# Another draw of the order table of a sparse-attention and gated-FFN kernel

## The chip, the cores and the metric

The kernel runs on one core of a Trainium2 chip, as one program. The metric is the device time of one execution in microseconds (us). The engines have short names here: PE (TensorE, matrix products and transposes), DVE (VectorE), ACT (ScalarE), POOL (GpSimd) and SP (SyncE, which here only issues transfers). POOL issues transfers too. The notes `u0` to `u7`, `x`, `g` and so on are the program's own names.

## The reference

Two layers stand one behind the other. The first is causal attention over 4 batches, 8 heads, 768 positions and 64 values per head. For each query only six chunks of 32 keys count. They are chosen by an upper bound, which is worked out from the minimum and the maximum of each chunk's keys.

```python
k_min = np.min(k_chunks, axis=3)
k_max = np.max(k_chunks, axis=3)
ub = np.sum(np.maximum(q * k_min, q * k_max), axis=-1)      # shapes cut
ub = np.where(causal, ub, -1000000000.0)
top_chunks = np.argsort(ub, axis=-1)[..., -top_k:]          # top_k = 6
scores = scale * np.matmul(q, k.transpose(0, 1, 3, 2))
scores = np.where(sel & (pos[:, None] >= pos[None, :]), scores, -1000000000.0)
attn = softmax(scores)
x = np.matmul(attn, v)                                      # to 3072 x 512
```

The second is a gated feed-forward layer on the 3072 tokens, from 512 to 1536 and back to 512.

```python
gate = 1.0 / (1.0 + np.exp(-(x @ w_gate)))
val = x @ w_val
return (gate * val @ w_out).astype(np.float32)
```

## The kernel before

**Units.** The tokens are cut into eight units of 384 tokens, three blocks of 128 each. Unit `u0` holds the first block of batches 0, 1 and 2, where no choice of chunks is needed. `u1` and `u2` hold the rest of batch 0 (and the first block of batch 3), `u3` and `u4` batch 1 (and one block of batch 2), `u5` to `u7` the rest.

**Stages of a unit.** Each stage is a few small operations with names of the form `kind_unit_part`.

- `first` (lines 560 to 650) does the first blocks. For a batch `b`: `kfT_b` and `qfT_b` turn keys and queries on PE, `kf16_b` and `qf16_b` copy them out of PSUM as half floats, `scf_b` makes scores, `expf_b_e` (ACT) exponentiates, `cmf_b_e` (POOL) applies the causal mask, `pvf_b_e` multiplies by the values, `rzf` and `xf` divide, `xpsf_b_e` turns the result and `xTf_b_e` copies it to `xT`, the input of the feed-forward layer. The loads are `kf0_b`, `kf1_b`, `qf0_b`, `qf1_b` (128 KB each) and `vf_b` (256 KB).
- `keys_wide` and `queries_wide` prepare `u1` and `u2`. The loads `k0_u1` to `k3_u1` and `q0_u1` to `q3_u1` bring 192 KB each. `kn` and `qn` copy a loaded piece, `kT` and `qT` turn it on PE, `kx` takes minimum and maximum, `kt` and `hk` put the keys in place for the scores, `qf`, `qm` (the positive part) and `hq` do the same for the queries. For the other batches `keys_blocks` and `turn_queries` do this with DVE's own transposes.
- `choose` makes the bounds: `ub` on PE, `ubn`, `mx` (the eight largest) and `ap` on DVE, then `apt`, and `hqm` copies the choice into the part of `hq` that adds a penalty to the scores. `hkp` fills the opposite part of `hk` with the pattern `epat` once, at the start.
- `attend` does, for each head, scores (`sc`), `exp` on ACT, the mask `cm` on POOL, and `pv`; `finish` divides and turns (`rz`, `x`, `xps`, `xT`).
- `ffn` does, for each of twelve parts of 128, a gate product `g`, `tanh`, a value product `v` and their product `hg` on DVE; `project_out` follows with `o0`, `o1`, `o2`, the copy `osb` and the store `out`. `u5` and `u6` share a version with fewer products (`ffn_pair`).

**Weights.** `w_gate`, `w_val` and `w_out` are loaded in three parts each (`wg0` to `wg2`, `wv0` to `wv2`, `wo0` to `wo2`, 512 KB each) by POOL. `after0` and `after1` are copies of one word on POOL, which read the second half of the queries of batch 1 and of batch 2. `wg0` and `wv0` depend on `after0`, the other parts on `after1` (lines 472 to 487 hold these). So the weights wait for the first loads.

**What sets the order.** All operations are first recorded in a `Plan`, with the buffers that they read and write. Nothing is scheduled by a rule then: `Plan.order` reads the string `ORDER`, one word per operation, and hands the operations out in that order. A word is the operation's name; `@ENGINE` names an engine where it isn't the first of those that the operation allows; after a colon stand the numbers of the buffers of a kind (PSUM banks among them) that the operation takes. Each engine runs its own operations in the order of the table and waits at each for what it needs; SP's loads run in the order of their words too. An operation that comes to a buffer later than another holds it from then on, so that the numbers set what has to wait for what.

Words of the same operations can be read in the table of either kernel: `qn_u1_2@POOL:4` is the copy of the third piece of `u1`'s queries, on POOL, into buffer 4 of its kind. At the end of the program the loop `for op in plan.order(): op.emit(op.engine)` emits all 1784.

Of the kernel before, what the change touches and what calls it, by code (L numbers as in the profile page):

```python
# [109 lines left out]
hq1_u1_2@POOL hq0_u1_2 qm_u1_3 v_u0_6:5 hq0_u1_3@DVE qf_u1_1 kcr_u1 tanh_u0_6 hg_u0_5 hq1_u1_3@POOL g_u0_7:7,3,7  # L110
hq1_u1_1@DVE qm_u1_1@ACT v_u0_7:6 hq0_u1_1@DVE tanh_u0_7 hg_u0_6 ub_u1:0,2 hg_u0_7 g_u0_8:4,0,8 ubn0_u1:0 ubn1_u1
v_u0_8:1 tanh_u0_8 ubm0_u1 k1_u2 ubm1_u1 v16_0_1 mx0_u1:0 g_u0_9:3,1,9 k2_u2 mx1_u1 v_u0_9:7 tanh_u0_9 g_u0_10:5,2,10
ap0_u1 ap1_u1 hg_u0_9 v_u0_10:6 tanh_u0_10 apt1_u1:0 g_u0_11:0,3,11 apt0_u1 hqm1_u1_2@DVE hqm1_u1_0@ACT v_u0_11:2
hqm0_u1_0@DVE tanh_u0_11 hqm0_u1_2@DVE sc_u1_0_1:4,3 sc_u1_1_0:3,0 hg_u0_10 exp_u1_0_1 sc_u1_0_0:7 o0_u0_0:5,0
# [5 lines left out]
exp_u1_4_1 kx1_u2_1:0 qn_u2_1@POOL:6 pv_u1_0 kf0_3:2 kt_u2_3:0 kx0_u2_2 hk0_u2_2@POOL pv_u1_3 exp_u1_4_2 qT_u2_0:7  # L120
rz_u1_0:0 hk0_u2_3 kf1_3 qn_u2_3:2 sc_u1_5_1:2,1 kx0_u2_3 hk1_u2_2@POOL sc_u1_6_2:6,3 o1_u0_1 qf_u2_0:1 kx1_u2_3
qn_u2_2@POOL:1 exp_u1_5_1 x_u1_0:0 hq1_u2_0@POOL qm_u2_0@ACT:0 qf0_3:3 qT_u2_2:7 v16_0_4 exp_u1_6_2 kx1_u2_2
sc_u1_4_0:0 hq0_u2_0 vf_3:4 sc_u1_5_2:2 qf_u2_2@DVE sc_u1_6_0:3 hk0_u2_1@POOL qT_u2_3:6 exp_u1_4_0 rz_u1_1:1 kT_u2_0:1
qm_u2_2 qT_u2_1:7 x_u1_1:1 hq1_u2_2@POOL qf_u2_3 o2_u0_1 kt_u2_0:2 cm_u1_4 qf_u2_1@DVE qf1_3 qm_u2_3@ACT kx1_u2_0
hq1_u2_3@POOL exp_u1_6_0 xps_u1_1:0,1 kx0_u2_0 k00_1:0 hq0_u2_1@POOL pv_u1_4:6 hq1_u2_1 sc_u1_5_0:5 osb_u0_1@DVE
hk1_u2_0@POOL sc_u1_6_1:7 xT_u1_1@ACT o0_u0_2:3,0 kcr_u2@POOL cm_u1_6 exp_u1_5_0 qm_u2_1 exp_u1_6_1 kfT_3:1
hq0_u2_3@DVE hq0_u2_2@DVE hk0_u2_0@ACT ub_u2:4,0 hk1_u2_3 kf16_3:4 cm_u1_5 exp_u1_5_2 out_u0_1 v16_0_5 vc_3@ACT
pv_u1_6:5 ubn1_u2:0 pv_u1_5 k01_1 sc_u1_7_0:7,2 ubn0_u2 sc_u1_7_2:1 sc_u1_7_1:2 mx1_u2:0 exp_u1_7_0 qfT_3:0 exp_u1_7_2
o1_u0_2 mx0_u2 cm_u1_7 exp_u1_7_1 qf16_3:5 ap1_u2 pv_u1_7 ap0_u2 o2_u0_2 apt1_u2:0 k10_1 rz_u1_3:0 rz_u1_2:1
hqm1_u2_0@DVE hqm1_u2_2@ACT scf_3:4,7,0 x_u1_3:2 sc_u2_4_2:1,3 osb_u0_2 xps_u1_0:2 x_u1_2:1 xps_u1_3:0 exp_u2_4_2  # L130
xT_u1_0 xps_u1_2:5 expf_3_1:1 xT_u1_3 sc_u2_7_2:3,2 xT_u1_2 expf_3_0 apt0_u2 sc_u2_7_1:6 cmf_3_1 g_u1_0:1,1,12
exp_u2_7_2 hqm0_u2_2@DVE exp_u2_7_1 v_u1_0:2 hqm0_u2_0@DVE out_u0_2 cmf_3_0 tanh_u1_0 k11_1 pvf_3_1:0 g_u1_1:7,2,13
hg_u1_0 rzf_3_1:0 pvf_3_0:5 v_u1_1:4 xf_3_1:0 tanh_u1_1 rzf_3_0:1 xf_3_0:2 sc_u2_3_0:3,0 sc_u2_3_2:6 hg_u1_1
xpsf_3_1:1,0 exp_u2_3_0 sc_u2_3_1:2 q00_1:1 xTf_3_1 xpsf_3_0:0 g_u1_2:7,3,14 exp_u2_3_2 xTf_3_0 cm_u2_3 exp_u2_3_1
# [15 lines left out]
o2_u1_1 hqm0_u3_0@DVE exp_u3_6_1 hqm0_u3_2@DVE sc_u3_1_2:1,0 sc_u3_0_2:0,1 osb_u1_1 sc_u3_0_0:2 out_u1_0 pv_u2_7  # L150
exp_u3_1_2 xps_u2_2:4 q00_2:1 xps_u2_1:7 rz_u2_3:1 exp_u3_0_2 xT_u2_2 sc_u3_5_2:5,2 exp_u3_0_0 x_u2_3:1 sc_u3_0_1:3
xT_u2_1 exp_u3_5_2 xps_u2_3:1 sc_u3_1_1:0 cm_u3_0 exp_u3_0_1 xT_u2_3 sc_u3_1_0:4 exp_u3_1_1 sc_u3_6_0:6 pv_u3_0:2
exp_u3_1_0 sc_u3_5_0:7 out_u1_1 kx1_2_0:0 k16_2_0:6 exp_u3_6_0 sc_u3_3_0:5,1 exp_u3_5_0 q01_2 o0_u1_2:1,1 cm_u3_1
# [1046 lines left out]
```

## Time and profile before

| what | value |
|---|---|
| three runs | 295.46, 293.73, 294.32 us |
| median | 294.32 us |
| profiled execution, span | 292.6 us |
| busy PE, DVE, ACT, POOL | 274.8, 219.8, 207.1, 94.6 us |
| first gate product (g_u0_0) | 22.71 us after the start |
| bytes moved by transfers | 32.69 MB |

The span runs from the first to the last instruction of one profiled execution; the runs' times contain what lies around it. Each engine's busy time is a sum over its instructions. The page's second part divides the span into 40 equal slices of some 7.3 us and gives each a digit, the busy share in tenths; the clock row gives the clock that PE was granted in the same way. Other views list the chain of work that ended last, the instructions in order of time, the busy time in chosen stretches, and the transfers by queue.

### The profile page before, as it was taken

Reading aid. Unit: us, or ns where it says so; the run is one execution under the profiler, and the core shown is the slowest. Engines: PE = TensorE matmul, PEld = TensorE weight load, DVE = VectorE, ACT = ScalarE, POOL = GpSimd, SP = SyncE. Lnnn points to the kernel's source line nnn. Section 1 sums busy time; section 2 is a strip of 40 time slices with the busy share of each in tenths; the row PEclk is TensorE's granted clock in tenths of the full one; section 3 lists DMA queues with packets and bytes.
Section 4 is the critical chain, followed back from the end, with each engine's and each line's share of the span. In section 5 each row is a group of like instructions: output and inputs, shape, how many; then the busy total and the mean of one; then the engine's idle time right before and its main releaser. Section 6 shows DMA issues by size and latency. Waiting matters only on the chain.

```text
span 292.6 us, 7019 instructions
## 1 busy us (share of the span) xinstructions
PE 274.8 (94%) x2644; PEld 175.0 (60%) x2644; DVE 219.8 (75%) x617; ACT 207.1 (71%) x425; POOL 94.6 (32%) x165
## 2 busy tenths in 40 slices
...
PEclk9985999999999999999999999999999999999999
...
GB/s 164 241 188 220 196 196 224 226 190 181 183 183 138 192 134 203 86 48 187 172 223 132 38 52 23 2 3 0 70 40 3 2 0 0 2 75 61 81 1 108
DMA packets 123377, 32.69 MB, mean 112 GB/s; under 512 B 111440, under 2 KB 120400, under 8 KB 123344
## 3 DMA queue, kind: packets, MB, share of 16 engines
...
## 4 chain that ended last, share of the span: by engine, by line
PE 83%; DMA 5%; ACT 4%; DVE 4%; POOL 2%; issue 1%; POOLq 0%
PE o_u L938 19%; PE v_u L907 16%; PE g_u L907 15%; PE sc_u L824 11%; PE pv_u L857 6%; DMA wv<-in_moe_w_val_dram 5%; PE sug_u5u L1016 3%; PE suv_u5u L1016 3%; PE ube_u L763 2%; ACT att_u L835 2%; PE xps_u L884 2%; PE srg_u5u L1016 1%; PE srv_u5u L1016 1%; DVE hko L331 1%; PE qT_u L662 1%
## 5 line engine op out<-in xcount | busy, mean ns | idle before, releaser
L835 ACT ACTIVATE att_u<-sc_u 128x512 f16<-128x512 f32 (+3 forms) x184 | 89.9, 549 | 15.1 <-PE sc_u L824 14.6
L919 DVE SCALAR_TENSOR_TENSOR hg_u<-gate_u,v_u 128x384 f16<-128x384 f16 x72 | 38.5, 542 | 33.7 <-PE v_u L907 25.2
L841 POOL TENSOR_SCALAR_AFFINE_SELECT att_u<-att_u 128x384 f16<-128x384 f16 (+1 forms) x56 | 29.3, 529 | 103.0 <-ACT att_u L835 100.8
L907 PE MATMUL v_u<-xT_u,wv 128*128 128x384 f16 x288 | 59.7, 331 | 2.5 <-DMA wv<-in_moe_w_val_dram 2.5
L907 PE MATMUL g_u<-xT_u,wg 128*128 128x384 f16 x288 | 59.9, 331 | 0.4 <-DVE xT_u L331 0.4
L938 PE MATMUL o_u<-wo,hg_u 128*128 128x512 f16 (+1 forms) x252 | 59.8, 376 | 0.0
L915 ACT ACTIVATE gate_u<-g_u 128x384 f16<-128x384 f32 x72 | 35.5, 493 | 28.6 <-PE g_u L907 21.8
L907 PEld LDWEIGHTS <-wv 128*128 128x128 f16 x288 | 27.8, 99 | 20.3 <-DMA wv<-in_moe_w_val_dram 3.2
L938 PEld LDWEIGHTS <-hg_u 128*128 128x128 f16 x264 | 24.6, 98 | 23.0 <-issue 0.6
L907 PEld LDWEIGHTS <-wg 128*128 128x128 f16 x288 | 27.4, 99 | 17.2 <-issue 2.5
L824 PE MATMUL sc_u<-hqo,hko 128*128 128x128 f16 (+2 forms) x220 | 28.5, 243 | 0.4 <-ACT att_u L835 0.4
L857 PEld LDWEIGHTS <-att_u 128*128 128x128 f16 x640 | 25.0, 98 | 5.5 <-issue 1.6
L857 PE MATMUL pv_u<-v,att_u 128*128 128x65 f16 x640 | 27.3, 193 | 0.0
L824 PE MATMUL sc_u<-hqe,hke 128*128 128x128 f16 (+2 forms) x220 | 26.4, 243 | 0.0
L947 ACT ACTIVATE osb_u<-o_u 128x512 f32<-128x512 f32 (+1 forms) x22 | 13.2, 599 | 18.6 <-PE o_u L938 18.6
L824 PEld LDWEIGHTS <-hke 128*128 128x128 f16 x220 | 16.8, 98 | 6.5 <-issue 0.4
L824 PEld LDWEIGHTS <-hko 128*128 128x128 f16 x220 | 16.5, 98 | 6.2 <-issue 1.2
L540 POOL CAST v<-v 128x512 f16<-128x512 f32 x23 | 15.0, 658 | 0.4 <-DMA v<-in_v_dram 0.2
L876 DVE TENSOR_TENSOR x_u<-pv_u,rz_u 128x384 f16<-128x384 f32 (+1 forms) x28 | 14.5, 527 | 0.2
L786 DVE MAX8 mx_u<-ubn_u 128x8 f32<-128x8 f32 (+16 forms) x152 | 12.5, 158 | 0.1
L714 DVE STREAM_TRANSPOSE kt<-k 128x768 f16<-128x768 f16 x12 | 11.5, 956 | 0.0
L548 DVE TRANSPOSE_TENSOR_REDUCE kx<-k 128x24 f32<-128x768 f32 x12 | 11.4, 947 | 0.0
(169 smaller groups left out, 446.8 us busy)
## 6 DMA issues: line engine op xcount, KB each, us to landing
...
```

The source lines that it names most:

```text
L540: plan.add(f"v16_{b}_{ib}", {POOL: pool(H * D)}, lambda e: nc.gpsimd.tensor_copy(v16[b % 2][:, ib, :, 0:D], at(t)), reads=[t], writes=[("v ...
L824: nc.tensor.matmul(at(t)[:, o:o + 128 * m], hk[b % 2][e_][:, p, 128 * jb:128 * jb + 128], hq[u.side][e_][:, p, 128 * x:128 * (x + m)], sta ...
L835: plan.add(f"exp_{u.name}_{h}_{y}", {ACT: act(n)}, lambda e, t=t, att=att, b0=b0, n=n: nc.scalar.activation(at(att)[:, b0:b0 + n], at(t), ...
L841: nc.gpsimd.affine_select(out=dv, in_=dv, compare_op=ALU.is_ge, fill=0.0, base=0, pattern=[[0, u.m], [1, 128]], channel_multiplier=-1)
L857: nc.tensor.matmul(at(pv)[:, last, x, :], at(att)[:, c:c + 128], v16[b % 2][:, jb, h, :], start=(jb == 0), stop=(jb == ib))
L876: plan.add(f"x_{u.name}_{p}", {DVE: dve(u.t)}, lambda e: nc.vector.tensor_tensor(at(x_).rearrange("p a (e d) -> p e a d", e=2), at(pv)[:, ...
L907: nc.tensor.matmul(at(t), w16[:, c, 128 * fb:128 * fb + 128], at(u.xt)[:, c, :], start=(c == 0), stop=(c == 3))
L915: plan.add(f"tanh_{u.name}_{fb}", {ACT: act(T)}, lambda e, g=g, gate=gate: nc.scalar.activation(at(gate), at(g), AF.Tanh, scale=0.5), read ...
L919: plan.add(f"hg_{u.name}_{fb}", {DVE: dve(T)}, lambda e, w_=w_, gate=gate, hg=hg: nc.vector.scalar_tensor_tensor(at(hg), at(gate), 1.0, at ...
L938: nc.tensor.matmul(at(o), hgs[c][1][1]()[:, 128 * tb:128 * tb + 128], wo16[:, fc, lo:hi], start=(c == 0), stop=(c == NFB - 1))
L947: nc.scalar.activation(at(osb)[:, lo:hi], at(o), AF.Copy, scale=0.5) if e == ACT
L1016: nc.tensor.matmul(at(t), left[i](c), right[i](c), start=first and c == 0, stop=c == 1, skip_group_check=not first)
```

## The change

Only the string `ORDER` is replaced. The words name the same 1784 operations; their order is different, 697 of them have other buffer numbers, and many have another engine. The rest of the program is the same, its lines one further down, since the new table has one line more.

By engine, the number of operations on POOL goes from 159 to 186, on DVE from 471 to 453, on ACT from 424 to 415. PE and SP have the same operations as before. Among the moves: eight `qm` go to POOL, which had none; POOL does eleven `hqm` where it did two; several `hq` go to POOL; of the copies `xT` eleven go from DVE to ACT and four the other way; of the copies `E` eleven go from ACT to DVE and six the other way; five `osb` go from ACT to DVE.

The start of both tables:

```diff
-vf1_3:0 kf0_0:0 ident kcr0 epat0:0 kf1_0 vf1_2:1 v10 ident16 ap1 epat qf1_0:1 ap0 qf0_0 hq1 kcr1 vf_0:2 hq0 v11
-kf1_1:3 hkp111 kf0_1 hkp110 hkp011@ACT kfT_0:0 qf1_1:4 hkp010 qf0_1 hkp000 hkp100@ACT qfT_0:1 kf16_0@DVE:2 vf1_1:3
-qf16_0:4 kxf0 hkp001@POOL hkf0@ACT kf1_2:5 kxf1:0 scf_0:2,3,1 v16_0_0 qf0_2:0 hkf1@ACT kcr_f kf0_2 hkp101 kfT_1:4
-expf_0_0 qf1_2 expf_0_1:2 after0 cmf_0_0 kf16_1@DVE:5 vf_1:1 qfT_1:5 cmf_0_1 vf_2:2 pvf_0_0:6 wg0 qf16_1:6 rzf_0_0:0
-pvf_0_1:7 xf_0_0:0 rzf_0_1:1 scf_1:1,0,3 wv0 xf_0_1:1 xpsf_0_0:2,0 expf_1_1:0 xTf_0_0 xpsf_0_1:3 expf_1_0 xTf_0_1
-cmf_1_1 cmf_1_0 k1_u1:0 k0_u1 kfT_2:4 k3_u1 after1 wg1 qfT_2:5 kf16_2:4 wv1 q0_u1 vc_1@ACT qf16_2@DVE:2 q2_u1 wg2
-pvf_1_0:6 pvf_1_1:7 k2_u1 rzf_1_0:0 scf_2:2,0,1 vc_2@ACT xf_1_0:2 wv2 q3_u1 rzf_1_1:1 expf_2_1:2 xpsf_1_0:3 xf_1_1:0
-wo0 xTf_1_0 expf_2_0 xpsf_1_1:1 xTf_1_1 cmf_2_1 cmf_2_0 pvf_2_1:4 q1_u1 kn_u1_1:5 rzf_2_1:0 wo1 pvf_2_0:5 v_0_1:3
-xf_2_1:1 kn_u1_0:6 kT_u1_1:6 rzf_2_0:1 xf_2_0:2 wo2 xpsf_2_1:7 kT_u1_0:0 kt_u1_1:0 xTf_2_1 kx0_u1_1 hk0_u1_1@ACT
-hk1_u1_1@POOL xpsf_2_0:3 xTf_2_0 kt_u1_0:1 kx1_u1_1:1 g_u0_0:2,0,0 hk1_u1_0 hk0_u1_0@ACT kx1_u1_0 v_u0_0:1 tanh_u0_0
...
-tanh_u0_2 v_u0_2:6 kt_u1_3:2 qT_u1_0:2 kx1_u1_3 hk0_u1_3@ACT hk1_u1_3@POOL g_u0_3:0,3,3 hg_u0_2 qf_u1_0:0 v_u0_3:1
-kx0_u1_3 qm_u1_0@ACT:0 hq0_u1_0@POOL hq1_u1_0 g_u0_4:4,0,4 tanh_u0_3 tanh_u0_4 hg_u0_3 qn_u1_2@POOL:4 v_u0_4:5 v_0_3:5
...
+ident q3_u1:0 kcr0 k3_u1 ident16 epat0:0 kf1_0:0 epat kf0_0 k1_u1 vf_0:1 qn_u1_3:0 qf0_0:2 qf1_0 vf_1:3 kfT_0:0
+kf0_1:4 kn_u1_1@POOL:1 qT_u1_3:1 v10 kf16_0:2 kf0_2:5 kn_u1_3@POOL:3 kT_u1_1:2 qf_u1_3@DVE:0 vf1_1:4 kf1_1 v16_0_0
+hkp110 kt_u1_1:0 qf1_2:0 hkp010@POOL qfT_0:3 hkp011@ACT kx0_u1_1 qf1_1:1 kxf0 qf0_1 kxf1:0 qf16_0:5 k0_u1
+hk0_u1_1@POOL q1_u2:1 scf_0:4,5,1 kf1_2 kfT_1:6 expf_0_1:2 after1 q0_u1 expf_0_0 cmf_0_1 q1_u1 kf16_1@DVE:6 qfT_1:7
+cmf_0_0 qf0_2 kx1_u1_1:1 kn_u1_0:0 after0 vf_2:2 vc_1 hkp100 pvf_0_1:1 kT_u1_0:0 q2_u1 wg0 kfT_2:3 qf16_1@DVE:1 k2_u1
+v_0_2:4 qm_u1_3@POOL:0 pvf_0_0:5 qn_u1_1:5 v_0_1:1 kT_u1_3:4 hq0_u1_3 wv0 scf_1:6,2,3 k1_u2 kt_u1_3@DVE:1 kcr_f@POOL
+expf_1_0 rzf_0_1:0 rzf_0_0:1 hq0 hkp000 cmf_1_0 qn_u1_2:0 kcr1 expf_1_1:1 xf_0_0:0 hq1_u1_3@POOL kx1_u1_3 qn_u2_1:3
+kf16_2:1 qT_u1_1:7 pvf_1_0:6 cmf_1_1 kx1_u1_0 hk1_u1_1@ACT kx0_u1_3 qT_u1_2:5 vf1_2:6 hkf0 vc_2@ACT xf_0_1:1 pvf_1_1:2
+wg1 rzf_1_0:0 xf_1_0:2 kt_u1_0@DVE:2 wv1 ap1 qf_u1_2@DVE qfT_2:3 qf16_2:5 qf_u1_1 scf_2:4,1,3 xpsf_0_1:6,0 qm_u1_1@ACT
+xpsf_0_0:3 qn_u1_0@POOL:0 xTf_0_0@ACT xpsf_1_0:7 expf_2_0 hk1_u1_3 hq0_u1_2@DVE xTf_0_1@ACT qT_u1_0:5 cmf_2_0
+expf_2_1:2 rzf_1_1:0 xf_1_1:1 hkp101@ACT kx0_u1_0 cmf_2_1 xpsf_1_1:3 pvf_2_0:4 xTf_1_0 rzf_2_0:0 wg2 pvf_2_1:6
+rzf_2_1:1 xf_2_1:0 kn_u1_2:4 wv2 xf_2_0:2 v_0_3:3 xpsf_2_1:1 xTf_1_1 qT_u2_1:2 xTf_2_1@ACT xpsf_2_0:0 wo0 qf_u1_0
+kT_u1_2:7 qm_u1_2@ACT qm_u1_0 kt_u1_2:0 xTf_2_0 k2_u2 kx1_u1_2 g_u0_0:6,0,0 ap0 kx0_u1_2 v_u0_0:4 hq0_u1_1@DVE
+kcr_u1@POOL g_u0_1:3,1,1 hk0_u1_3@POOL ub_u1:1,5 hkp001@POOL tanh_u0_1 tanh_u0_0 hq0_u1_0 hg_u0_0 v_u0_1:0 wo1
...
```

In the new table, seven turns of `u1` and `u2` (`kT_u1_3`, `kT_u1_2`, `qT_u1_0` to `qT_u1_3`, `qT_u2_1`) stand ahead of `g_u0_0` that stood behind it; `ub_u1` follows `g_u0_1` where it followed `v_u0_7`; and the loads of `first` and of `u1` are mixed.

More of the change, by code (lines that the diff above doesn't have):

```diff
@@ L110 @@
[L110 to L114, printed above, removed]
@@ L120 @@
[L120 to L124, printed above, removed]
@@ L125 @@
[L125 to L134, printed above, removed]
@@ L150 @@
[L150 to L153, printed above, removed]
-kx0_2_0 exp_u3_3_0 k16_2_2:4 pv_u3_1 kx1_2_1 k16_2_1@ACT:5 sc_u3_3_1:3 o1_u1_2 cm_u3_5 exp_u3_3_1 cm_u3_6 kt_2_2:2
@@ new lines @@
+qm_u2_0@ACT kf16_3@DVE:0 exp_u1_6_2 kcr_u2@POOL vc_3@ACT ub_u2:5,3 osb_u0_1@DVE xps_u1_2:1 pv_u1_6:6 ubn1_u2:0 v_0_5:4
+xT_u1_2@ACT scf_3:2,0,3 mx1_u2:0 pv_u1_7 hq1_u2_0 o0_u0_2:7,0 expf_3_0 ap1_u2 hk0_u2_2@ACT rz_u1_3:0 ubn0_u2 o1_u0_2
+cmf_3_0 apt1_u2:0 x_u1_3:1 v_0_4:1 hqm1_u2_2@ACT hqm1_u2_0 o2_u0_2 mx0_u2 q10_1:1 hk1_u2_2@POOL hq1_u2_3 xps_u1_3:4
+expf_3_1:2 ap0_u2 sc_u2_7_1:3,0 xT_u1_3 sc_u2_4_2:1,1 osb_u0_2 v_1_2:3 pvf_3_0:2 apt0_u2 sc_u2_7_2:5 g_u1_0:6,1,12
+k16_1_3:6 rzf_3_0:0 exp_u2_4_2 kx1_1_1:1 hqm0_u2_2@ACT v_u1_0:0 cmf_3_1 xf_3_0:0 exp_u2_7_2 g_u1_1:4,0,13 kx1_1_2
@@ new lines @@
+xps_u3_3:4 sc_u4_0_1:6 osb_u2_1@DVE xT_u3_3@ACT cm_u4_1 sc_u4_2_2:7 ub_u5:5,2 xT_u3_2 exp_u4_2_2 v16_2_4 ap1_u4
+exp_u4_0_1 cm_u4_2 exp_u4_0_3 apt1_u4 k16_3_1@ACT:5 sc_u4_1_1:4 hq0_u5_2@POOL kt_3_0:3 o0_u2_2:0,1 hqm1_u4_0 ubn0_u5:0
+pv_u4_0:1 o1_u2_2 kx0_3_2 sc_u4_1_3:7 sc_u4_4_0:6,2 hq0_u5_0 exp_u4_4_0 sc_u4_2_3:3 o2_u2_2 ubn1_u5 exp_u4_1_3
+mx0_u5:0 exp_u4_2_3 sc_u4_4_3:5 g_u3_0:6,1,17 osb_u2_2 exp_u4_1_1 v_u3_0:2 mx1_u5 out_u2_2 k16_3_3@ACT:4 out_u2_1
+sc_u4_4_2:7 g_u3_1:3,0,2 ap0_u5 v_3_4:2 hqm1_u4_2@DVE pv_u4_1 v_3_3:4 ap1_u5 tanh_u3_1 sc_u4_3_0:0 tanh_u3_0 rz_u4_0:0
```

264 lines of the change are left out of this document (139 added, 125 removed).

## The prediction

> **What bounds the kernel now.** I read the head of the page first, then its slices.
>
> ```profile
> span 292.6 us, 7019 instructions
> PE 274.8 (94%) x2644; PEld 175.0 (60%) x2644; DVE 219.8 (75%) x617; ACT 207.1 (71%) x425; POOL 94.6 (32%) x165
> PEclk9985999999999999999999999999999999999999
> ```
>
> TensorE (PE) is busy for 94% of the span, the other engines for at most 75%. The clock row names the exception: the fourth slice has half the clock. So I cut the span at the first gate product (22.7 us) and at the points where the pace changes. The columns are the length, then busy time of PE, PEld, DVE, ACT and POOL, the granted clock, the DMA share and GB/s.
>
> ```profile
> 0.00:22.70 22.70, 12.36 (x90) 9.13 (x91) 16.06 (x39) 13.78 (x21) 16.50 (x33) 0.94 0.94 199
> 22.70:30.60 7.90, 5.36 (x18) 2.34 (x18) 2.81 (x6) 1.89 (x4) 0.34 (x1) 0.52 1.20 215
> 30.60:66.60 36.00, 36.00 (x370) 23.75 (x369) 29.39 (x110) 28.73 (x70) 14.76 (x31) 1.00 1.09 206
> 66.60:170.00 103.40, 102.52 (x1110) 66.51 (x1116) 96.31 (x260) 84.84 (x169) 47.87 (x77) 1.00 0.79 148
> 170.00:190.00 20.00, 19.16 (x247) 12.18 (x232) 19.77 (x87) 15.34 (x31) 7.58 (x11) 1.00 0.07 25
> 190.00:252.60 62.60, 62.60 (x622) 41.39 (x621) 45.20 (x101) 49.01 (x107) 7.51 (x14) 1.00 0.04 14
> 252.60:289.40 36.80, 36.80 (x209) 19.73 (x206) 10.26 (x20) 13.25 (x26) 0.00 (x0) 1.00 0.15 58
> ```
>
> From 30.6 us on PE has no idle time but 0.88 us in the fourth row and 0.84 us in the fifth, 1.7 us together; in the fifth DVE is busy for 19.77 of 20 us. What a new order can gain or lose therefore lies in two places: before 30.6 us, and in whether the later rows stay full. The chain of waits and then the timeline show the early part (start, duration, what; in brackets the idle time before it and what ended it).
>
> ```profile
> 12.89 13.74 DMA wv<-in_moe_w_val_dram
> ...
> 28.14 1.28 PE g_u L907 x4
> 29.42 1.11 PE v_u L907 x4
> 33.13 0.65 PE v_u L907 x4
> 37.23 0.65 PE qT_u L662 x6
> ...
> 288.74 0.68 PE ob_u L938 x12
> ```
>
> ```profile
> 11.97 0.93 POOL L479 DMA_DIRECT2D wg<-in_moe_w_gate_dram  x1
> 22.71 1.44 PE L907 MATMUL g_u<-xT_u,wg 128*128 128x384 f16 x4 [0.38 <-DVE xT_u L331]
> 26.68 1.46 PE L907 MATMUL v_u<-xT_u,wv 128*128 128x384 f16 x4 [2.53 <-DMA wv<-in_moe_w_val_dram]
> ```
>
> The first gate product starts at 22.71, the first value product waits 2.53 us for its weights, and four products run at about half pace (1.44, 1.46, 1.28 and 1.11 where 0.65 is the full-pace price). From 22.71 to the end of PE's work at 289.42 are 266.7 us.
>
> **The change part by part.** The same 1784 operations remain, so PE's work is the same, and so is the code that each emits. Three things move.
>
> *First, PE's order at the start.* Ahead of g_u0_0 there now also stand kT_u1_3, kT_u1_2, qT_u1_0 to qT_u1_3 and qT_u2_1. Six transposes of 128 columns take 0.65 us (the qT_u row above), so six turns of three and one of two are 2.2 us of later work brought forward. The order after some 40 us of PE's work is nearly the old one: g_u1_0 and g_u7_0 stand behind the same amount of PE work to within 0.1 us, and the tail is unchanged.
>
> *Second, SP's queue.* The old order loaded the fifteen pieces for `first` (kf, qf, vf) ahead of u1's eight. The new one mixes them. q2_u1 is now the 23rd load, with 3776 KB up to its end, and its users come early: on ACT qn_u1_2 stands ahead of expf_1_1, and on PE qT_u1_2 stands ahead of pvf_1_1, qfT_2 and scf_2, and so ahead of everything that leads to g_u0_0. Before, qn_u1_2 ran on POOL and had nothing of `first` behind it. This is a new wait, and its queue is the path to the first weight product. When does q2_u1 land? The transfers in three windows (queue: packets, MB, share of the engines; 2 to 14, 16 to 24, 28 to 46 us):
>
> ```profile
> q1 hardware_dynamic: 10054, 2.81, 99.4%
> ```
>
> ```profile
> q0 software_dynamic: 1020, 1.02, 79.0%
> q1 hardware_dynamic: 920, 0.67, 35.7%
> ```
>
> ```profile
> q0 software_dynamic: 2813, 2.80, 91.4%
> q1 hardware_dynamic: 2811, 0.72, 29.9%
> ```
>
> q1 carries SP's loads, q0 the weights that POOL issues. Alone, q1 moves 0.234 MB/us from about 2 us on; beside the weights 0.084 with packets of 768 bytes (16 to 24) and 0.040 with those of 256 bytes (28 to 46). Free of weights, q2_u1's 3.87 MB would be in at 2 + 3.87/0.234 = 18.5 us. The first weight transfer waits for after1 and after0, which read qf_2 and qf_1; qf1_1 is now the 14th load (2.29 MB, in at 11.8). Behind it POOL still has two masks and a cast:
>
> ```profile
> 6.51 0.62 POOL L540 CAST v<-vf 128x512 f16<-128x512 f32 x1 [0.27 <-DMA vf<-in_v_dram]
> 13.86 1.22 POOL L620 TENSOR_SCALAR_AFFINE_SELECT attf<-attf 128x512 f16<-128x512 f16 x2 [0.22 <-ACT attf L618]
> ```
>
> So wg0's issue moves from 11.97 to about 11.8 + 1.22 + 0.62 = 13.7, and the crowding, which I put at 2.5 us behind the issue, to 16.2. By then q1 has moved 3.32 MB. What is left are 0.35 MB of 256-byte packets (vf_2 above all) and q2_u1's 0.20 MB. At 0.040 and 0.084 MB/us these take 8.7 and 2.3 us: 27.2. Undisturbed it is 18.5. I take the mean of the two crowded rates for the first part (0.062: 5.6 us), because only two weight transfers are in flight then where the row of 28 to 46 had more: L = 24.1.
>
> From that landing the chain to g_u0_0 runs through these durations (rows of the timeline, in the order of the new chain; a row of x2 holds two operations):
>
> ```profile
> 17.91 0.93 ACT L329 COPY kn_u<-kq_u 128x384 f32<-128x384 f32 x2
> 13.19 1.08 ACT L618 ACTIVATE attf<-scf 128x512 f16<-128x512 f32 x2 [1.18 <-DVE xf L635]
> 19.58 0.30 PE L627 MATMUL pvf<-vf,attf 128*128 128x65 f16 x4 [1.80 <-POOL attf L620]
> 14.25 1.06 PE L576 MATMUL qfT<-ident,qf 128*128 128x128 f32 x4
> 11.43 0.58 ACT L329 CAST qf<-qfT 128x512 f16<-128x512 f32 x1 [0.21 <-PE qfT L576]
> 12.40 0.61 PE L613 MATMUL scf<-qf,kf 64*128 64x128 f16 x8
> 16.95 0.28 PE L642 MATMUL xpsf<-ident,xf 128*128 128x128 f16 x2
> 4.14 1.47 ACT L329 COPY hko<-epat 64x1536 f16<-64x1536 f16 x1 [0.77 <-POOL epat L443]
> 20.38 0.88 PE L662 MATMUL kT_u<-ident,kn_u 128*128 128x128 f32 x3
> ```
>
> qn 0.47 (as kn), exp 0.54, mask 0.61, pvf 0.30, qfT 1.06, cast 0.58, scf 0.61, two xpsf 0.56. Then ACT, in its order, has two copies to xT (at most 0.48 each), two exps (0.54 each), the fill hkp101 (1.47) and kn_u1_2 (0.47). Last kT_u1_2, 0.88. The sum is 9.6; some fifteen hand-overs (scf ends at 13.01, its exp starts at 13.19) add about 0.9. So g_u0_0 starts at 24.1 + 10.5 = 34.6, not 22.71.
>
> *Third, engines.* Nine more of the `hqm` copies, eight `qm` and several `hq` go to POOL, some casts and copies change between ACT and DVE.
>
> ```profile
> L331 DVE COPY hqe<-apt_u 64x768 f16<-64x768 f16 x6 | 2.4, 394 | 0.1
> L333 POOL COPY hqo<-apt_u 64x768 f16<-64x768 f16 x1 | 1.1, 1082 | 1.6 <-DVE apt_u L797 1.6
> L333 POOL CAST hqe<-qf_u 64x768 f16<-64x768 f32 x5 | 4.2, 848 | 10.7 <-DVE qf_u L730 10.7
> ```
>
> An `hqm` costs 1.08 us on POOL and 0.39 on DVE. No row has `qm` on POOL; its bounds are 0.85 (the cast with the same columns) and twice that, and I take the upper, since the operation is another. By such prices some 25 us come onto POOL, 4 leave DVE and 7 ACT. POOL had 94.6 busy, so this lies beside PE's work as long as each copy is there before its scores. Where the cover ends, the third rival prices it. The gain is at most the 1.7 us that PE idled in the fourth and fifth rows, the loss bounded there; I take 1.2 of gain, nearer to its upper end because the idle time stands where DVE was full.
>
> **The sum.** Of the old 266.7 us, 2.5 go (the wait for wv0: now issued at about 15.7 and 13.74 on its way, it lands at 29.4, ahead of 34.6) and 2.7 (the four slow products: 0.79 + 0.81 + 0.63 + 0.46), and 2.2 were brought forward: 259.3. After a sparse start PE comes back at half clock as the second row of the stretches shows; four to five us at half pace, mostly filled, cost 2.0 (1 to 3). End of PE: 34.6 + 259.3 + 2.0 - 1.2 = 294.7, against 289.4: 5.3 later. That makes the span 297.9. The median of the runs, 294.32, lies 1.7 above the span, so the time is **299.6**.
>
> **The rivals.** *Crowding from the first byte.* The 28-to-46 row has as many packets on one queue as on the other (2813, 2811). If one weight transfer is enough for that share, L is 27.2, 3.1 later: 302.7. For it speaks the equality; against it that in 16 to 24 the counts were 1020 and 920 at other packet sizes, with q1 still at 0.084 MB/us. In the Trainium skill, "DMA: Bandwidth & Descriptors", section "Queues, rings and completion order", each DMA engine takes turns between the queues it has work for, a packet at a time; by that rule this rival holds, and the equal counts agree with it.
>
> *Faster.* If wg0's packets come later than I reckon, or q2_u1 passes before them, L is 18.5 and g_u0_0 starts at 28.1 to 29.0; then wv0, 13.74 us behind an issue at about 15.7, is just in. The end is 5.6 to 6.5 earlier than in my sum; with the whole 1.7 of idle time gained and 1 us of half pace it is 291.5 to 292.5. For it speaks that only 0.55 MB are in question, and that u1's own preparation, which PE, DVE and ACT must do anyway, then stands ahead of the weights' arrival. Against it: all sixteen DMA engines are busy from 2 us on, and this needs wg0's issue to slip by 2 us.
>
> *No change.* With L near 20 the two effects cancel: 295.
>
> *POOL becomes the bound.* In u1 to u4 the `hqm` on POOL is queued 1.2 to 1.5 us of PE work ahead of the scores that need it. If POOL is late there, nine copies at 0.7 us more and no relief elsewhere give 299.6 + 1.2 + 6.2/2 = 304. Against it: POOL's 47.87 of 103.40 us. In the Trainium skill, "SBUF — State Buffer", section "SBUF: two separate sides", POOL and some forms of DVE instructions hold a shared port one at a time, the other fully blocked. By that rule the 25 us more on POOL would also stretch DVE. The fourth row has DVE and POOL at 96.31 + 47.87 in 103.40 us, so at least 41 us lie side by side, if a blocked instruction isn't counted as busy.
>
> That the table might do nothing is excluded: the order of every queue differs.
>
> **How the numbers follow.** Forecast 0.44 (its own range 297 to 302), crowding from the first byte 0.14, POOL 0.1: slower 0.68. Faster 0.2. No change 0.12. About 0.5% is what a measurement of this kernel can tell. The range holds 8 in 10 if it reaches from the faster case's lower half to between the two late ones: 291.5 to 304.
>
> **What would show it.** In the changed kernel's trace: q2_u1 landing near 24; qn_u1_2 on ACT waiting for that DMA, and behind it a stretch of 4 to 8 us in which PE has little work; g_u0_0 near 34.6, with three or four products slower than 0.65 behind it, and no wait for wv0; hardly any idle time of PE after 45 us. It would be wrong if g_u0_0 started before 30 us, if PE had gaps of more than 2 us in the stretch that was full, or if a score waited for a copy on POOL.

## The result, and the profile after

| kernel | median | spread | ratio to before (95% interval) |
|---|---|---|---|
| before | 294.02 us (4 runs) | 293.73 to 295.46 | 1 |
| changed | 298.07 us (4 runs) | 296.65 to 298.5 | 1.0136 [1.0097, 1.0174] |
| changed, measured again with the last experiments | 297.15 us (7 runs) | 294.06 to 298.11 | 1.0093 [1.0059, 1.0128] |

The changed kernel is about 1% slower. The ratios leave out the few runs that were clearly slower than the others of the same kernel; the longest, 480 us at a mean granted clock of 0.57, is one of the kernel without seventeen copies on POOL, below. The head of its page and its clock row, to be held against those of before:

```profile
span 295.5 us, 6996 instructions
PE 275.5 (93%) x2644; PEld 176.7 (60%) x2644; DVE 215.6 (73%) x599; ACT 200.3 (68%) x416; POOL 122.2 (41%) x192
PEclk9995699999999999999999999999999999999999
```

DVE has 4 us less, ACT 7 us less, POOL 28 us more, and the span is 2.9 us longer. The fourth slice still shows half the clock, and now the fifth shows 0.6 of it. The busy time in stretches (columns as above: length, PE, PEld, DVE, ACT, POOL, clock, DMA share, GB/s), cut at the first gate product, which now starts at 32.49:

```profile
0.00:32.49 32.49, 17.27 (x110) 13.05 (x111) 17.75 (x41) 17.01 (x31) 19.44 (x37) 0.82 1.03 211
32.49:40.20 7.71, 7.71 (x66) 3.95 (x66) 5.13 (x22) 2.26 (x6) 3.10 (x5) 0.87 1.21 221
40.20:70.00 29.80, 29.59 (x301) 19.45 (x300) 22.67 (x80) 24.69 (x59) 15.78 (x33) 1.00 0.93 166
70.00:100.00 30.00, 28.68 (x292) 18.49 (x290) 27.40 (x76) 22.09 (x45) 15.86 (x25) 1.00 1.03 192
100.00:170.00 70.00, 70.00 (x745) 45.91 (x744) 61.61 (x172) 55.60 (x115) 45.50 (x63) 1.00 0.68 133
170.00:190.00 20.00, 20.00 (x281) 12.70 (x280) 17.90 (x67) 14.88 (x28) 11.27 (x12) 1.00 0.11 41
```

Up to the first gate product PE now has 17.27 us of work in 32.49 us, where it had 12.36 in 22.70, and the mean clock of that stretch is 0.82 instead of 0.94. After it PE is full but for 0.21, 1.32 and, further on, 0.04 us: 1.6 us, about the 1.7 of before. The chain of waits names what came last in the start, and the timeline shows the instructions at that place:

```profile
13.76 8.28 DMA kq_u<-in_q_dram
...
32.49 1.44 PE g_u L908 x4
...
291.66 0.68 PE ob_u L939 x12
```

```profile
13.85 0.99 POOL L480 DMA_DIRECT2D wg<-in_moe_w_gate_dram  x1
15.85 0.81 POOL L481 DMA_DIRECT2D wv<-in_moe_w_val_dram  x1
...
22.11 0.51 ACT L330 COPY qn_u<-kq_u 128x384 f32<-128x384 f32 x1 [3.86 <-DMA kq_u<-in_q_dram]
22.53 0.59 ACT L619 ACTIVATE attf<-scf 128x512 f16<-128x512 f32 x1
22.68 0.50 PEld L663 LDWEIGHTS qT_u<-ident,qn_u 128*128 128x128 f32 x3 [3.43 <-ACT qn_u L330]
22.68 0.90 PE L663 MATMUL qT_u<-ident,qn_u 128*128 128x128 f32 x3 [3.31 <-ACT qn_u L330]
23.02 0.40 ACT L330 COPY qn_u<-kq_u 128x256 f32<-128x256 f32 x1
23.25 0.64 POOL L621 TENSOR_SCALAR_AFFINE_SELECT attf<-attf 128x512 f16<-128x512 f16 x1 [3.67 <-ACT attf L619]
```

q2_u1 was issued at 13.76 and landed 8.28 us later, at 22.04. ACT stood idle for 3.86 us ahead of qn_u1_2, PE for 3.31 ahead of qT_u1_2, POOL for 3.67 ahead of cmf_1_1: one late transfer holds three engines, because its user stands in the middle of the chain of `first` on two queues. From there the chain runs to g_u0_0 without a longer pause.

The account of the two profiled executions: g_u0_0 starts 9.78 us later (32.49 against 22.71); from there to PE's end are 259.85 us (292.34 - 32.49) instead of 266.7, 6.85 less. The difference is the 2.9 us of the spans.

### The profile page after: what moved, and what is told of

Same layout as the page of the kernel before. It is cut to its first block, busy times and chain, and to the rows that moved or that the text cites. A ratio compares the mean times of both kernels' runs of the same rounds, so it can differ in the third digit from the quotient of the medians.

```text
span 295.5 us, 6996 instructions
## 1 busy us (share of the span) xinstructions
PE 275.5 (93%) x2644; PEld 176.7 (60%) x2644; DVE 215.6 (73%) x599; ACT 200.3 (68%) x416; POOL 122.2 (41%) x192
## 4 chain that ended last, share of the span: by engine, by line
PE 84%; DMA 5%; SPq 4%; ACT 2%; POOL 2%; issue 1%; DVE 1%; ACTq 0%; DVEq 0%; POOLq 0%
PE o_u L939 21%; PE g_u L908 15%; PE v_u L908 15%; PE sc_u L825 11%; PE pv_u L858 6%; DMA kq_u<-in_q_dram 3%; PE suv_u5u L1017 3%; PE sug_u5u L1017 3%; PE ube_u L764 3%; SPq L504 2%; DMA q<-in_q_dram 2%; PE xps_u L885 2%; PE srg_u5u L1017 1%; PE srv_u5u L1017 1%; POOL qm_u L565 1%; SPq L515 1%
## 5 line engine op out<-in xcount | busy, mean ns | idle before, releaser
L836 ACT ACTIVATE att_u<-sc_u 128x512 f16<-128x512 f32 (+3 forms) x184 | 92.1, 547 | 22.6 <-PE sc_u L825 20.0
L842 POOL TENSOR_SCALAR_AFFINE_SELECT att_u<-att_u 128x384 f16<-128x384 f16 (+1 forms) x56 | 28.5, 519 | 82.4 <-ACT att_u L836 68.8
L920 DVE SCALAR_TENSOR_TENSOR hg_u<-gate_u,v_u 128x384 f16<-128x384 f16 x72 | 37.6, 543 | 30.7 <-PE v_u L908 15.6
L916 ACT ACTIVATE gate_u<-g_u 128x384 f16<-128x384 f32 x72 | 34.2, 497 | 21.3 <-PE g_u L908 18.7
L825 PE MATMUL sc_u<-hqo,hko 128*128 128x128 f16 (+2 forms) x220 | 30.1, 243 | 0.0
L825 PE MATMUL sc_u<-hqe,hke 128*128 128x128 f16 (+2 forms) x220 | 29.1, 243 | 0.0
L948 ACT ACTIVATE osb_u<-o_u 128x512 f32<-128x512 f32 (+1 forms) x17 | 9.9, 590 | 19.8 <-PE o_u L939 19.8
L825 PEld LDWEIGHTS <-hko 128*128 128x128 f16 x220 | 17.4, 98 | 7.1 <-issue 0.5
L565 POOL TENSOR_SCALAR qm_u<-qf_u 128x768 f32<-128x768 f32 (+3 forms) x8 | 14.1, 1766 | 5.6 <-DVE qf_u L731 3.5
L731 DVE STREAM_TRANSPOSE qf_u<-q 128x384 f32<-128x384 f32 (+2 forms) x28 | 11.2, 436 | 3.3 <-DMA q<-in_q_dram 3.3
```

Source lines behind the costliest of these rows:

```text
L565: (nc.vector if e == DVE else nc.gpsimd).tensor_scalar_max(o, i, 0.0)
L825: nc.tensor.matmul(at(t)[:, o:o + 128 * m], hk[b % 2][e_][:, p, 128 * jb:128 * jb + 128], hq[u.side][e_][:, p, 128 * x:128 * (x + m)], sta ...
L836: plan.add(f"exp_{u.name}_{h}_{y}", {ACT: act(n)}, lambda e, t=t, att=att, b0=b0, n=n: nc.scalar.activation(at(att)[:, b0:b0 + n], at(t), ...
L842: nc.gpsimd.affine_select(out=dv, in_=dv, compare_op=ALU.is_ge, fill=0.0, base=0, pattern=[[0, u.m], [1, 128]], channel_multiplier=-1)
L916: plan.add(f"tanh_{u.name}_{fb}", {ACT: act(T)}, lambda e, g=g, gate=gate: nc.scalar.activation(at(gate), at(g), AF.Tanh, scale=0.5), read ...
L920: plan.add(f"hg_{u.name}_{fb}", {DVE: dve(T)}, lambda e, w_=w_, gate=gate, hg=hg: nc.vector.scalar_tensor_tensor(at(hg), at(gate), 1.0, at ...
```

## The experiments

All times are medians; ratios are to the kernel before, measured beside each. An edit names the words of the table that are moved.

**A load exchanged.** SP's queue alone is changed.

```diff
-... expf_0_1:2 after1 q0_u1 expf_0_0 ...
+... expf_0_1:2 after1 q2_u1 expf_0_0 ...
-... pvf_0_1:1 kT_u1_0:0 q2_u1 wg0 ...
+... pvf_0_1:1 kT_u1_0:0 q0_u1 wg0 ...
```

> The changed kernel with two words exchanged in the table: q2_u1 takes the place of q0_u1 in SP's queue (19th load, 3008 KB to its end) and q0_u1 the 23rd. In the changed kernel q2_u1 landed at 22.04 us, qn_u1_2 ran at 22.11 and g_u0_0 started at 32.49. If the late load is what the start waits for: q2_u1 lands at 2 + 3.08/0.234 = 15.2, qn_u1_2 runs at about 18.3 behind expf_1_0 and doesn't wait; the next late load is q0_u1 at about 22 for qn_u1_0, from whose end 6.0 us led to g_u0_0: g_u0_0 at 28.6, the time 3.9 us shorter than the changed kernel's, 294.2. If the start is bound by the work brought forward (the turns on PE) or by the weights instead, g_u0_0 stays above 31 and the time within 1.5 us of 298.1.

Measured: 292.62 us, 0.9962 [0.9941, 0.9983], span 291.1. The rows of its timeline:

```profile
17.77 0.51 ACT L330 COPY qn_u<-kq_u 128x384 f32<-128x384 f32 x1
...
22.40 0.50 POOL L334 COPY qn_u<-kq_u 128x384 f32<-128x384 f32 x1 [0.37 <-PE scf L614]
...
28.22 1.44 PE L908 MATMUL g_u<-xT_u,wg 128*128 128x384 f16 x4
```

qn_u1_2 runs at 17.77 with no wait ahead of it, g_u0_0 starts at 28.22 (28.6 was expected), and the span is 4.4 us shorter than the changed kernel's. That the late load held the start is shown; the sum that gave 28.6 is not. It ran over q0_u1, which landed at 22.28, but the chain of waits in this profile doesn't pass there: it runs from the landing of q1_u1 (16.36) over its copy and the masks on POOL. Two words decide whether the new table is slower than the old one or, by 0.4%, faster.

**The load one place later.**

```diff
-... kT_u1_0:0 q2_u1 wg0 kfT_2:3 qf16_1@DVE:1 k2_u1 ...
+... kT_u1_0:0 k2_u1 wg0 kfT_2:3 qf16_1@DVE:1 q2_u1 ...
```

> The changed kernel with q2_u1 and k2_u1 exchanged in SP's queue, so that q2_u1 is the 24th load, one load of 192 KB later. If its landing sets the start one for one: it lands at about 24.2 (2.2 us later, the pace of such loads beside the weights), g_u0_0 starts at 34.7, and the time is about 2.2 us longer, 300.3. If the start has another bound, g_u0_0 stays within 0.7 us of 32.49 and the time is the changed kernel's.

Measured: 298.99 us, 1.0168 [1.0124, 1.0212], span 297.6. From the chain of waits:

```profile
15.44 8.96 DMA kq_u<-in_q_dram
...
34.86 1.44 PE g_u L908 x4
```

The landing moved to 24.40, g_u0_0 to 34.86, the span by 2.1 us. The median rose by 0.9 us only, where 2.2 were expected; the profiles show the step more plainly than the times, because the landing differs from one execution to the next. Over the runs in which q2_u1 is the gate, the distance from the start of qn_u1_2 to that of g_u0_0 doesn't change at all: 22.11 to 32.49 (10.38) in the changed kernel, 24.47 to 34.86 (10.39) here, 20.88 to 31.27 (10.39) in the changed kernel's second profile, 22.02 to 32.42 (10.40) in the experiment on qm_u3 below.

**The users exchanged instead of the loads.** SP's queue is the changed kernel's; the words of piece 0 and piece 2 change places for qn, qT, qf and hq0, with their engines.

```diff
-... cmf_1_0 qn_u1_2:0 kcr1 ... qT_u1_2:5 ... qf_u1_2@DVE ... qn_u1_0@POOL:0 ... qT_u1_0:5 ... qf_u1_0 ...
+... cmf_1_0 qn_u1_0:0 kcr1 ... qT_u1_0:5 ... qf_u1_0@DVE ... qn_u1_2@POOL:0 ... qT_u1_2:5 ... qf_u1_2 ...
```

> The changed kernel with its loads as they are, but the early users exchanged: qn, qT, qf and hq0 of piece 0 take the places of those of piece 2, so that the operation on ACT ahead of expf_1_1 needs q0_u1 (landed at 16.06 in the changed kernel) and q2_u1 (22.03) is needed only by the copy on POOL behind wv1. If the place of the late load's user is what cost the time, this gives the same as moving the load: g_u0_0 near 28.3, the time 4 to 5 us shorter than the changed kernel's 298.1, q2_u1 still landing near 22. If the transfers themselves or the work brought forward cost it, the time stays within 1 us of the changed kernel's.

Measured: 293.2 us, 0.9961 [0.9929, 0.9994], span 291.3; g_u0_0 at 27.76, q2_u1 landing at 21.68. The load is nearly as late as before, and PE's first gate product is 4.7 us earlier: its user now runs on POOL at 22.51, without a wait, and of `first` only the masks of batch 2 stand behind it there. So a late landing costs this time only through the place of its user in the queues.

**The weights held back.** wg0 and wv0 stand behind cmf_1_1 on POOL.

```diff
-... kT_u1_0:0 q2_u1 wg0 kfT_2:3 ... hq0_u1_3 wv0 scf_1:6,2,3 ... cmf_1_1 kx1_u1_0 ...
+... kT_u1_0:0 q2_u1 kfT_2:3 ... hq0_u1_3 scf_1:6,2,3 ... cmf_1_1 wg0 wv0 kx1_u1_0 ...
```

> The changed kernel with wg0 and wv0 on POOL moved behind cmf_1_1, so that no weight is on its way while q2_u1 is. If the weights' packets are what slows q2_u1, it lands at about 18.5 instead of 22.04, with the same queue ahead of it; if the queue alone makes it late, it stays within 0.5 us of 22. The weights then come later: wg0 issued near 20.4, in at 28 to 30, wv0 at 30 to 33, so g_u0_0 starts at 29 to 30 and v_u0_0 may wait for wv0; the time is 0 to 3 us shorter than the changed kernel's.

Measured: 296.83 us, 1.0078 [1.0039, 1.0117]. The timeline of this kernel:

```profile
18.06 0.51 ACT L330 COPY qn_u<-kq_u 128x384 f32<-128x384 f32 x1
...
28.86 1.46 PE L908 MATMUL g_u<-xT_u,wg 128*128 128x384 f16 x4 [0.48 <-DMA wg<-in_moe_w_gate_dram]
33.23 1.46 PE L908 MATMUL v_u<-xT_u,wv 128*128 128x384 f16 x4 [2.90 <-DMA wv<-in_moe_w_val_dram]
```

With the same queue ahead of it, q2_u1 landed at 17.98 and its user didn't wait; the weights on their way made it 4 us late. But now the weights are late: v_u0_0 waits 2.90 us for wv0, the wait that the old table had too. The interval of the ratio overlaps the changed kernel's, so no gain is shown. The transfers between 18 and 22 us, the changed kernel first:

```profile
q0 software_dynamic: 521, 0.52, 78.1%
q1 hardware_dynamic: 687, 0.40, 37.9%
```

```profile
q1 hardware_dynamic: 3537, 1.05, 109.5%
```

Beside the weights SP's queue got 0.40 MB through in these 4 us, without them 1.05 MB.

**Two copies off POOL.** qm_u3_0 and qm_u3_2 back on DVE and ACT.

```diff
-... hg_u1_5 qm_u3_2@POOL:0 tanh_u1_7 ... k10_2 qm_u3_0@POOL rz_u2_1:0 ...
+... hg_u1_5 qm_u3_2@ACT:0 tanh_u1_7 ... k10_2 qm_u3_0 rz_u2_1:0 ...
```

> The changed kernel with qm_u3_0 and qm_u3_2 back on the engines that they had before (DVE and ACT; 0.72 and 0.86 us there, 1.80 us each on POOL in the changed kernel). In the changed kernel PE is idle for 1.3 us between 70 and 100 us, ahead of ub_u3, and the chain of waits runs through the load of q_1 (landing at 87.1), then qm_u3 on POOL twice. If POOL's price makes that gap, it goes away and the time is 1.3 us shorter, 296.8. If the load of q_1 makes it, more than 0.8 us of the gap stay. If DVE and ACT are too full to take the two, the time stays or grows by up to 0.5.

Measured: 297.97 us, 1.0106 [1.0059, 1.0153]. In 85 to 95 us (the changed kernel, then this one):

```profile
85.00:95.00 10.00, 8.68 (x95) 4.70 (x92) 7.92 (x22) 6.72 (x13) 6.95 (x9) 1.00 1.02 178
```

```profile
85.00:95.00 10.00, 8.88 (x102) 5.43 (x101) 8.46 (x22) 7.35 (x14) 5.02 (x9) 1.00 1.08 187
```

PE still idles 1.1 us of the 1.3. The two copies are faster, but they now stand in line with tanh and hg, and PE waits for those (0.6 and 0.5 us). So taking POOL's price of 1.8 us away doesn't close the gap. That fits both of the last two outcomes named beforehand and doesn't tell them apart.

**The load of q_1 earlier.** On top of the first experiment, q01_1 ahead of a store.

```diff
-... sc_u2_4_0:6 out_u0_2 pv_u2_3:1 ... sc_u2_0_1:6 q01_1 v_u1_5:3 ...
+... sc_u2_4_0:6 q01_1 pv_u2_3:1 ... sc_u2_0_1:6 out_u0_2 v_u1_5:3 ...
```

> The first experiment (q2_u1 for q0_u1; g_u0_0 at 28.22, span 291.1) with one exchange more in SP's queue: q01_1, the last quarter of q_1, ahead of the store out_u0_2. In the changed kernel q01_1 was issued at 81.44 behind that store, landed at 87.09, and PE idled 1.3 us in 85 to 95 behind it; the last experiment on qm_u3 left that gap. If the late load makes the gap, the load comes about 2 us earlier, the gap falls below 0.4 us, and the time is about 1 us shorter than the first experiment's 292.6. If the gap stays as it is, something else on SP or DVE sets ub_u3.

Measured: 292.91 us, 0.9969 [0.9941, 0.9997]: no gain. q01_1 was issued at 75.64 and landed 6.84 us later, at 82.48, where the first experiment had 77.33 + 5.37 = 82.70. An earlier issue bought 0.2 us, so the time of issue doesn't set the end of this load; that the transfers themselves do is likely and not shown. The gap is 0.7 us in 80 to 100, where the first experiment has 1.0, but between 100 and 120 us PE has a new wait:

```profile
PE g_u L908 <- DVE hg_u L920: 1.3, 1, 1.3
```

What would close the gap, and why this wait came, stays open.

**The nineteen moved qm and hqm off POOL.** The order is the changed kernel's; the engines of these operations, eight qm and eleven hqm, are those of the old table. (One more hqm was on POOL before and stays there: the new table has twelve, not eleven.)

```diff
-... qm_u1_3@POOL:0 ... hqm0_u1_2 ... qm_u2_3@POOL ... hqm0_u3_0 ... qm_u6_0@POOL ...
+... qm_u1_3:0 ... hqm0_u1_2@DVE ... qm_u2_3@ACT ... hqm0_u3_0@DVE ... qm_u6_0 ...
```

> The changed kernel with the 19 qm and hqm operations that it moved to POOL back on the engines that they had before; the order is kept. Eight qm (1.0 to 1.8 us on POOL in the changed kernel's trace) and eleven hqm leave POOL, some 22 us of its 122. If the engines' moves lie beside PE's work, as the prediction has them, the time is within 1 us of the changed kernel's 298.1. If POOL's slow copies cost PE waits, or its instructions slow DVE's, the time is 2 to 4 us shorter and the mean of DVE's groups falls (hg_u 543 ns). If the moves relieve full DVE and ACT, the time is 1 to 2 us longer, with PE idle in 70 to 190.

Measured: 300.75 us, 1.023 [1.0189, 1.0271]: slower than the changed kernel (1.0136 [1.0097, 1.0174]), though wv0 was issued at 14.96 and g_u0_0 started at 30.50 in its profile, 2 us earlier. PE's stretch after g_u0_0 had 262.5 us against 259.85.

To leave the start alone, seventeen of them (all but those of u1) went back on top of the first experiment:

> The first experiment with the 17 qm and hqm of u2 to u7 that the change moved to POOL back on the engines they had before; nothing in the start is touched, so g_u0_0 stays at about 28.2. From g_u0_0 to PE's end the first experiment had 259.7 us. If POOL's share relieves DVE and ACT, this stretch grows by 2 to 4 us with idle time of PE waiting for DVE or ACT, and the time is 295 to 297. If the moves lie beside PE's work and are worth nothing, the time stays within 1 us of 292.6. If POOL is a bound or slows DVE, it is shorter by 1 us or more.

Measured: 295.93 us, 1.0064 [1.004, 1.0088], 1% above the first experiment. Its trace is that of a further run:

> The kernel with the 17 later qm and hqm off POOL once more, for its trace. The timed runs gave 295.9, some 3 us above the first experiment. If DVE and ACT miss the relief, PE's stretch from g_u0_0 to its end is 262 to 263.5 (259.7 in the first experiment) and PE idles for 2.5 to 4 us in it, after DVE or ACT; if the time comes from elsewhere, the stretch is within 1 us of 259.7 and g_u0_0 is late instead.

Measured: 296.04 us (one run), span 294.3, g_u0_0 at 28.72, and PE's end at 291.16: 262.4 us, 2.7 more than the first experiment's 259.7. Two stretches of the first experiment, then of this kernel, and what PE waited for in the latter (engine, waiter, releaser; us, times, longest):

```profile
80.00:100.00 20.00, 19.03 (x188) 10.97 (x187) 18.18 (x60) 12.63 (x26) 14.35 (x20) 1.00 1.09 196
100.00:170.00 70.00, 70.00 (x809) 46.36 (x808) 60.97 (x171) 53.58 (x110) 43.19 (x57) 1.00 0.61 121
```

```profile
80.00:100.00 20.00, 18.42 (x187) 10.83 (x185) 17.78 (x59) 12.78 (x26) 8.81 (x16) 1.00 1.10 195
100.00:170.00 70.00, 68.70 (x725) 44.43 (x723) 61.19 (x175) 56.65 (x115) 32.95 (x49) 1.00 0.61 121
```

```profile
PE xps_u L885 <- DVE x_u L877: 0.8, 1, 0.8
PE g_u L908 <- ACT gate_u L916: 0.7, 1, 0.7
PE v_u L908 <- DVE hg_u L920: 0.5, 1, 0.5
PE sc_u L825 <- ACT att_u L836: 0.3, 1, 0.3
```

With 10 us less on POOL in 100 to 170, PE loses 1.3 us there that it didn't lose in the first experiment. This sum alone proves little: the kernel with q01_1 earlier, which keeps the copies on POOL, loses as much there, by its one wait for hg_u. What tells is that the waits of 0.8, 0.7 and 0.3 us stand, with the same sizes, in the profile with all nineteen off POOL too, and in no profile that keeps them all on POOL, and that both kernels are slower in their runs. So the copies on POOL are a relief of DVE and ACT in this order, worth some 3 us, and POOL isn't a bound.

**A shorter start.** On top of the first experiment.

```diff
-... scf_2:4,1,3 xpsf_0_1:6,0 ... xpsf_1_0:7 expf_2_0 hk1_u1_3 ... cmf_2_0 expf_2_1:2 ... hkp101@ACT ... kn_u1_2:4 ...
+... scf_2:4,1,3 expf_2_0 expf_2_1:2 xpsf_0_1:6,0 ... xpsf_1_0:7 hk1_u1_3 ... cmf_2_0 ... kn_u1_2:4 hkp101@ACT ...
-... xTf_1_1 qT_u2_1:2 xTf_2_1@ACT xpsf_2_0:0 wo0 ... kt_u1_2:0 xTf_2_0 ...
+... xTf_1_1 xTf_2_1@ACT xpsf_2_0:0 xTf_2_0 qT_u2_1:2 wo0 ... kt_u1_2:0 ...
```

> The first experiment (q2_u1 for q0_u1) with five words moved in the start: expf_2_0 and expf_2_1 right behind scf_2, hkp101 behind kn_u1_2, qT_u2_1 and xTf_2_0 behind and right behind xpsf_2_0. In the first experiment expf_2_0 stood 0.75 us behind two copies on ACT, and qT_u2_1 (0.6 us) between the last two xpsf. If the chain that follows the late load's user is the bound of g_u0_0, these two shorten it: g_u0_0 at about 27.0 instead of 28.22, the time 1.2 us shorter than the first experiment's 292.6, 291.4. If wv0 (issued at 15.9) isn't there by then, v_u0_0 waits for it and the time is the first experiment's.

Measured: 293.21 us, 0.9991 [0.9965, 1.0016], g_u0_0 at 28.57: no gain in time. The rows of scf_2, the first experiment's and then this kernel's:

```profile
21.70 0.61 PE L614 MATMUL scf<-qf,kf 64*128 64x128 f16 x8 [0.73 <-ACT qf L330]
23.01 0.61 PE L614 MATMUL scf<-qf,kf 64*128 64x128 f16 x8 [0.73 <-ACT qf L330]
```

From scf_2 to g_u0_0 are 5.56 us, where the first experiment had 6.52: the edit shortened what it touches by nearly 1.0 us (1.2 were expected). But scf_2 itself stood 1.3 us later in this execution, in the part that the edit leaves alone; there the load qf0_1, for one, landed at 13.10 instead of 12.61. The loads q0_u1 and k2_u1 landed 1.0 us later each (23.23 and 25.33), but the chain of waits doesn't run through them; from 17.8 to 26.9 us it runs mostly over DVE. Why the time of twelve runs shows nothing of the shorter stretch stays open. v_u0_0 didn't wait.

**The changed kernel once more.**

> The changed kernel as it is, in the same rounds as the other two, to have its time with a narrower interval: between 296.5 and 298.5, with q2_u1 landing between 21 and 23 and g_u0_0 10.4 us behind it.

Measured: 297.15 us, 1.0093 [1.0059, 1.0128]; q2_u1 landed at 20.81 (issued at 13.79, 7.02 on its way) and g_u0_0 started at 31.27. The landing is what varies between executions of this kernel, here by 1.2 us, and g_u0_0 moves with it.

## Why the prediction was right, step by step

- **The forecast.** 299.6 us was predicted; 298.07 was measured, and 297.15 with the last experiments: the first inside the forecast's own range of 297 to 302, the second at its edge, both slower than before. The mechanism, a late load whose user stands ahead of the chain of `first`, is shown by three experiments, which move the load earlier, move it later, and move its user. Part of the nearness is luck: the sum's span of 297.9 was 2.4 us too long (295.5), but the profiled execution took 298.28 us, 2.8 more than its span, where 1.7 were added.
- **L, the landing of q2_u1.** 24.1 was predicted; 22.04 and 20.81 were measured. The weights' issue came as worked out (13.85 for 13.7), and undisturbed the load lands at 17.98 (18.5). What was off was the crowded rate. In 16 to 18 us SP's queue still moved 0.21 MB, 0.105 MB/us, where the sum had 0.062; vf_2 was in at 17.9. So the first part took 1.7 us from 16.2 on, where the sum had 5.6. But q2_u1 itself then took 4.1 us where the sum had 2.3, since other loads of SP's queue moved beside it: it is only 0.20 of the 0.40 MB of 18 to 22 us. The two errors had opposite signs, and 2.1 us were left.

```profile
q0 software_dynamic: 192, 0.20, 72.8%
q1 hardware_dynamic: 820, 0.21, 46.0%
```

  These are the packets of 16 to 18 us: 192 against 820. The rival of full crowding from the first byte rested on equal counts, and it falls. In the Trainium skill, "DMA: Bandwidth & Descriptors", section "Queues, rings and completion order", the engines take turns between queues by packets. The counts of 18 to 22 us (521 and 687) are nearer to that, those of 16 to 18 us don't show it; whether the packets that the profile counts are the packets of that rule, no run here shows.
- **The chain.** 10.5 us from the landing to g_u0_0 was predicted; 10.45 was measured, and it repeats to 0.02 us in four profiles. That the sum hit it is in part luck, because its last steps were not on the path. Up to the end of the second exp of batch 2 it had about 7.5 us with the hand-overs; the trace has 6.8 (22.04 to 28.82), as some of these steps were shorter or overlapped. From there the sum went on with hkp101, kn_u1_2 and kT_u1_2, 2.8 us and hand-overs. In the trace kn_u1_2 ended at 30.83 and kT_u1_2 started only at 31.52, so that path had slack. The chain of waits goes through the rest of `first`, with two operations of u1 between, and takes 3.7 us (28.82 to 32.49):

```profile
28.30 0.51 ACT attf L619
28.87 0.65 POOL attf L621
29.56 0.41 PE pvf L628 x4
30.22 0.43 DVE xf L636
30.70 0.41 PE xpsf L643 x2
31.91 0.33 DVE qm_u L565
```

  So the wait and the head of the chain were right, and the tail was another one of nearly the same length.
- **The wait for wv0.** It went, as predicted: no profile of the changed kernel has it. The experiment with the weights held back shows what it costs when it returns.
- **Half pace.** 2.0 us (1 to 3) was taken. In the profile the clock was 0.87 over 7.71 us, 1.0 us; the second profile of the same kernel had 1 us more from g_u0_0 to PE's end (260.9 against 259.85). The clock record of the traces agrees: the half clock began well ahead of g_u0_0 in both (at 20.87 and 18.58) and lasted for 2.0 us behind it in the first and for 4.4 in the second, where the sum had four to five.
- **The engines.** The term of 1.2 us of gain fell: PE idles 1.6 us after its start where it idled 1.7. This and the half pace were off by about as much with opposite signs, so that the stretch after g_u0_0 came out at 259.85 for a predicted 260.1. What the experiments add is that the copies on POOL are needed: without them this order loses 2.7 us, more than the 1.7 that I gave as the bound of a loss.
- **The price of qm on POOL.** The upper bound of twice 0.85 us was too low:

```profile
L565 POOL TENSOR_SCALAR qm_u<-qf_u 128x768 f32<-128x768 f32 x4 | 8.6, 2157 | 2.5 <-PE ubo_u L764 1.9 <-DVE qf_u L731 0.6
L563 ACT ACTIVATE qm_u<-qf_u 128x768 f32<-128x768 f32 x2 | 1.7, 841 | 0.0
```

  2.16 us on POOL, 0.84 on ACT for the same form. It lay beside PE's work but for one wait: in the gap between 85 and 95 us, ub_u3 waited 0.5 us for qm_u on POOL.
- **The POOL rival.** It falls by its own sign: less on POOL was slower. In the Trainium skill, "SBUF — State Buffer", section "SBUF: two separate sides", POOL and certain DVE instructions lock each other out. The trace agrees. `ap` on DVE reads two tiles of SBUF; in the changed kernel it took 0.41 to 0.44 us in the three executions of this form that had no POOL instruction beside them, and 0.87 to 0.90 in the three that had one. The first row has none beside it, the second has three:

```profile
122.31 0.41 DVE L792 TENSOR_TENSOR ap<-ubn_u,mx_u 128x288 f16<-128x288 f32 x1
136.43 0.88 DVE L792 TENSOR_TENSOR ap<-ubn_u,mx_u 128x288 f16<-128x288 f32 x1
```

  The main operation of DVE, hg_u, which reads one input from PSUM, shows nothing of it: its mean is 543 ns with 122 us on POOL and 542 without the seventeen copies. What DVE loses in this way is less here than what the copies on POOL relieve.

```profile
L920 DVE SCALAR_TENSOR_TENSOR hg_u<-gate_u,v_u 128x384 f16<-128x384 f16 x72 | 37.6, 543 | 30.7 <-PE v_u L908 15.6 <-ACT gate_u L916 12.1 <-PE sc_u L825 1.6
```

- **The faster rival.** Its condition (q2_u1 there before the weights) was not met, but the first experiment makes it true by another way, and the time is then 292.6, close to the 291.5 to 292.5 that was worked out.
